# A third weight buffer for the last segment's projections, laid over the token tiles of the input norms, with a new table of shifts

## The chip, the cores and the metric

The kernel runs on one core of a Trainium2 chip. The metric is the device time of one execution in microseconds, the median of several runs. The profile is of one execution, taken by the hardware profiler; its times count from the first instruction. TensorE multiplies matrices (PE in the profile; PEld is its weight load), VectorE is DVE, ScalarE is ACT, GpSimd is POOL, and SyncE (SP) issues all transfers (DMA).

## The reference

One transformer block on 2048 tokens of width 1024: a layer norm, attention with a compressive memory, a residual, a second layer norm, a gated feed-forward of inner width 3584, a residual.

```python
h = x + A(layernorm(x))          # A: 32 heads of 32, 4 segments of 512 tokens
out = h + B(layernorm(h))

# A, for each segment s: causal attention inside the segment, and a memory of those before
p = softmax(q @ k.T * 32**-0.5 + mask); a_dot = p @ v
a_mem = (phi(q) @ M) / (phi(q) @ z + 1e-6)      # phi(t) = t + 1 if t > 0 else exp(t)
o = g * a_mem + (1 - g) * a_dot                 # g = sigmoid(beta), one for each head
M = M + phi(k).T @ v; z = z + sum(phi(k))
A = o @ wo

B = (silu(x @ w1) * (x @ w3)) @ w2
```

Inputs and weights are bfloat16.

## The kernel before, in words

**A planner writes the order.** The kernel builds a graph of operations (`Graph`), each with an engine or a choice of engines, a cost in the planner's own model, and the operations it depends on. `Graph.op` and `Graph._touch` find the dependences from the memory that operations read and write, so two tiles laid over the same place are kept apart automatically. `Graph.schedule` then plays the graph through: whenever an engine is free, it takes, among the operations that are ready, the one with the lowest pair of class (`cls`) and sequence number (`seq`). The result is a fixed order on each of the five queues (TensorE, ScalarE, VectorE, GpSimd, SyncE). `Graph.emit` writes it out with semaphore waits. On the chip nothing is reordered: a late transfer holds its queue up.

**Shifts.** Operations are counted in units: `Graph.stage` begins the next one. A table `SHIFT` gives a unit a pair (a number added to `seq`, a number added to `cls`). With it the order is moved about without touching the code that builds the graph. Classes: score bursts 0, columns and retrievals 1, projections 5, output projections 5 or 7, feed-forward up 7, feed-forward down 8; transfers have classes of their own. Units 252 to 281 are the projections of the last segment, segment 3. Unit 252 is the load of the first half of the query weights, and 253 to 256 are the four output tiles made with it; 257 with 258 to 261 are the same for keys, 262 with 263 to 266 for values; 267 to 281 repeat this for the second half.

**Stages.** `first_half` normalizes the first four token tiles and projects half of segment 0's queries, keys and values in short matmuls. `ln1(s)` loads the four token tiles of segment s into `xs0` to `xs3`, normalizes them in place (`ln`) and transposes them by DMA into `xnT[s]`. `qkv(s)` makes queries, keys and values with six weight halves of 1 MB: `weights` picks a buffer, a DMA fills it, and `project` runs four groups of eight matmuls of 512 columns. `attention` makes ten score bursts for each half of the heads (line 1101), each followed by an exponential on ScalarE (line 1115) and a causal mask on GpSimd (line 1124). `finish` makes numerators and denominators in column tiles (line 1194), the memory update (line 1029), and normalizes; for segments 2 and 3 the reciprocals go out to memory and come back spread over the partitions (`r_scr`, then `R0w` and `R`). `retrieve` reads the memory (line 1316). `wo_stage(s)` is the output projection with the second norm, whose result is transposed into `hnT[s]`. `ffn_up` and `ffn_down` are the feed-forward, in two blocks of 1024 tokens. Ordinary matmuls of all stages are recorded by one helper, `mms`, at line 747, so in the profile they are told apart by their tiles.

Projections, output projections and feed-forward matmuls are what TensorE does between the score bursts, which ScalarE's exponentials space out.

**Weight buffers.** `wp0` and `wp1` are places of their own; `wp2` lies on `oT1`, the attention output of odd segments, and so can be used by segments 0 and 1 only. `weights` counts its calls in `n_wp`, six for each segment: numbers 0 to 11 rotate over three buffers, 12 to 23 over `wp0` and `wp1`. The feed-forward's weight pairs, `w13[0]` = (`w1b0`, `w3b0`) and `w13[1]` = (`w1b1`, `w3b1`), lie at `r2` and `r2 + 8192`. At `r2` are the token tiles `xs0` to `xs3`, 2 KB each in a partition; at `r2 + 8192` is `xnT`, the normalized input of segments 0 and 3.

Of the kernel before, what the change touches and what calls it, by code (L numbers as in the profile page):

```python
# [10 lines left out]
BF16 = DT.bfloat16  # L11
# [19 lines left out]
    0: (-18, 0), 3: (-173, 0), 4: (-182, 0), 5: (1074, 0), 6: (1041, 1), 7: (-959, -1),  # L31
    8: (-283, 1), 9: (1560, 1), 10: (-14, 0), 11: (1, 0), 12: (51, -1), 13: (-257, 0),
    14: (-1703, 0), 15: (2952, 0), 16: (-2912, 0), 18: (-87, -1), 19: (3455, 1), 20: (-401, -1),
    21: (22, 0), 22: (2924, -1), 23: (-669, 0), 24: (-328, -1), 26: (-261, -1), 27: (11, -1),
    28: (-153, 0), 29: (-317, 0), 31: (1524, -1), 32: (211, 0), 33: (-1, 0), 34: (2, 0),
    35: (-15, 0), 38: (118, 1), 39: (2057, 0), 40: (223, 0), 41: (2279, -1), 42: (914, 1),
    43: (-1135, 1), 44: (2665, 1), 45: (3218, 1), 47: (1997, 1), 48: (664, -1), 49: (1928, -1),
    50: (-2800, -1), 51: (7, 0), 52: (-1130, 0), 53: (116, 0), 54: (669, 0), 55: (1018, 0),
    56: (2, 0), 57: (-289, 1), 58: (4, 0), 59: (731, 0), 60: (-304, 0), 61: (-436, 0),
    62: (64, 1), 63: (-3, 0), 64: (-63, 0), 65: (-50, 0), 66: (-174, 0), 67: (-937, 0),  # L40
    68: (808, 0), 69: (1512, -1), 70: (28, 0), 71: (-58, 1), 72: (1441, 1), 73: (-75, 1),
    74: (2141, 0), 75: (778, 1), 76: (-752, 1), 77: (90, 1), 78: (-21, 0), 79: (151, 0),
    80: (1343, 0), 81: (-1130, 0), 83: (160, 0), 84: (687, 0), 85: (-676, 0), 86: (312, 0),
    87: (-266, 0), 88: (-263, 0), 89: (-1189, -1), 90: (-164, 0), 91: (680, 1), 92: (-1801, 0),
    93: (1499, 0), 94: (3153, 0), 95: (-261, 0), 96: (0, -1), 97: (-11, 0), 98: (2, 0),
    99: (944, 0), 100: (-54, 0), 101: (1016, 0), 102: (-842, 0), 103: (147, 0), 104: (-1191, 0),
    106: (-47, 0), 107: (121, 1), 108: (-1142, 0), 109: (-1295, -1), 111: (699, 0),
    112: (-365, -1), 113: (-594, 0), 115: (28, 0), 116: (2452, -1), 117: (-8, 0), 118: (676, 0),
    119: (54, 0), 120: (-1449, -1), 121: (235, 0), 122: (-9, -1), 123: (-13, 1), 124: (45, 0),
    125: (-1279, 1), 127: (-283, -1), 129: (555, 0), 130: (1438, -1), 132: (617, 1),  # L50
    133: (81, 0), 134: (-2285, -1), 135: (-179, 0), 136: (3199, 1), 137: (389, 0),
    138: (920, 0), 139: (146, 1), 140: (687, 1), 141: (27, 0), 142: (-619, 1), 143: (1934, 1),
    144: (-922, 0), 145: (415, -1), 146: (-312, 0), 147: (-26, 0), 148: (-870, 0),
    149: (2501, 1), 150: (1682, 0), 151: (-28, 0), 152: (609, 1), 153: (611, 0), 154: (-302, 0),
    156: (0, 1), 157: (-185, 1), 158: (391, 0), 159: (-373, 0), 160: (-610, 0), 161: (-1748, 0),
    162: (-133, 0), 163: (-4056, 1), 164: (1073, 1), 166: (-202, 0), 168: (-3204, -1),
    169: (-2075, -1), 170: (2581, -1), 171: (-39, 1), 172: (-122, 1), 173: (-18, 1),
    174: (-37, 0), 175: (34, 0), 176: (1853, 1), 177: (-140, 0), 178: (-301, 0), 179: (204, 0),
    181: (165, 0), 182: (-13, 0), 183: (-7, 0), 184: (687, -1), 185: (-271, 0), 186: (-861, 1),
    187: (-616, 1), 188: (355, -1), 189: (-1449, 1), 190: (1132, 0), 191: (114, 0),  # L60
    192: (-22, 0), 193: (-464, 0), 194: (-2, 0), 195: (294, 0), 196: (18, 0), 197: (-2089, 0),
    199: (-2443, 0), 200: (248, -1), 201: (1, 0), 203: (210, 1), 204: (-1070, 0), 206: (-70, 0),
    207: (1441, 0), 208: (525, 0), 209: (839, 0), 210: (10, 0), 211: (-262, 0), 212: (894, -1),
    213: (203, 1), 214: (-359, 1), 215: (-2, 0), 216: (696, -1), 217: (-735, 0), 218: (-51, 0),
    219: (4750, 0), 220: (-465, -1), 221: (-23, 0), 222: (-196, 1), 223: (399, 0),
    224: (-1932, 1), 225: (-192, 0), 226: (-134, 0), 227: (-1542, 1), 229: (153, 1),
    230: (-676, 1), 231: (-73, 0), 232: (618, 1), 234: (-465, 0), 235: (0, -1), 237: (222, -1),
    238: (609, 0), 239: (1282, 0), 241: (-183, 1), 242: (845, 1), 243: (811, -1),
    244: (1681, -1), 246: (6, 1), 248: (-2423, -1), 249: (11, 0), 250: (21, 0), 251: (-2902, 1),
    252: (-599, 1), 253: (927, 0), 255: (308, -1), 256: (4, -1), 257: (-382, 0), 258: (30, 0),  # L70
    259: (-35, 0), 260: (-73, -1), 261: (-386, 0), 262: (-58, 1), 263: (-1713, 0),
    264: (-165, 0), 265: (-369, 1), 266: (-12, 0), 267: (808, -1), 268: (1356, 0),
    269: (-538, 0), 270: (576, -1), 272: (27, 0), 273: (609, 0), 275: (-27, 0), 277: (0, -1),
    279: (-4, 0), 280: (-3, 0), 281: (176, 0), 282: (-28, -1), 284: (-175, -1),
    285: (-1255, -1), 286: (-196, 0), 287: (308, 0), 288: (1028, 0), 289: (-18, 0),
    290: (-217, -1), 291: (628, 0), 292: (21, 0), 293: (11, 0), 294: (1042, 0), 295: (6, 0),
    296: (150, -1), 297: (222, 0), 298: (1329, 0), 299: (-799, 0), 300: (-3, 0), 301: (303, -1),
    302: (-473, -1), 303: (2419, -1), 304: (528, 0), 305: (-99, 0), 306: (2531, -1),
    307: (-28, 0), 309: (-1338, 1), 310: (-4, 1), 311: (836, 0), 312: (-154, 0), 315: (-261, 0),
    316: (443, 0), 317: (-31, -1), 318: (-1464, -1), 319: (-220, 0), 320: (340, 0),  # L80
    321: (1268, 0), 322: (-21, -1), 323: (-2755, 1), 324: (-54, 0), 325: (1643, -1),
    326: (-57, 0), 327: (1851, 0), 328: (-2912, 0), 329: (317, 1), 330: (-690, 0),
    331: (-712, -1), 332: (-940, 0), 333: (-1099, 1), 334: (-615, 1), 335: (-16, 0),
    336: (496, 0), 337: (664, 0), 338: (-166, 0), 339: (-46, 0), 340: (-700, 0), 341: (-385, 1),
    342: (-1713, 0), 344: (51, 0), 345: (-756, -1), 346: (178, -1), 348: (803, 0),
    350: (1942, -1), 351: (169, 0), 352: (-492, 1), 354: (14, 0), 355: (-39, 0), 356: (290, 0),
    357: (99, 0), 358: (-389, 0), 359: (1761, 0), 361: (1409, 0), 362: (-58, -1), 363: (550, 1),
    364: (-95, 1), 365: (-140, 1), 366: (56, 1), 367: (-11, 1), 368: (-1627, 0),
    369: (-393, -1), 370: (-2089, 0), 372: (27, 0), 373: (204, -1), 374: (-55, 0),
    375: (-622, 0), 376: (-1005, -1), 377: (-179, 0), 378: (-1188, 1), 379: (1478, -1),  # L90
    380: (-865, -1), 381: (-543, 0), 382: (-70, 0), 383: (-64, 0), 384: (-1160, 0),
    385: (-2800, 0), 386: (0, 1), 387: (-193, 1), 388: (-133, 0), 390: (2419, 0),
    391: (2201, -1), 392: (-35, -1), 394: (45, -1), 395: (-2041, 0), 396: (410, 0),
    397: (571, 1), 399: (-543, -1), 400: (-965, 0), 401: (2531, 0), 402: (-462, -1),
    403: (-129, 0), 404: (-89, 1), 405: (-60, -1), 407: (-887, 1), 408: (3072, 0),
    409: (3013, 0), 410: (1761, 1), 411: (1584, 0), 413: (281, 1), 414: (562, 0),
    415: (-1293, -1), 416: (1707, 0), 417: (-995, -1), 418: (1637, 0), 419: (-785, -1),
    420: (3, 0), 422: (-913, -1), 423: (-121, -1), 424: (-7, 0), 426: (-2, 0), 427: (-1, 0),
    430: (-1, 0), 431: (14, 0), 432: (8, 0), 433: (-33, 0), 435: (-1086, 0), 436: (72, 0),
    437: (51, -1), 438: (-293, -1), 439: (37, 1), 440: (1527, 1), 441: (-212, 0),  # L100
    442: (-3190, 1), 443: (-1357, -1), 444: (-520, 1), 445: (904, 0), 446: (-1018, -1),
    447: (697, 0), 449: (2458, 0), 450: (-40, 0), 451: (-44, 0), 452: (-8, 0), 453: (-14, 0),
    454: (658, -1), 455: (-3, 0), 456: (1, 0), 457: (-3, 0), 459: (-2315, 1), 461: (-1, 0),
    462: (539, 0), 463: (66, 0), 464: (788, 1), 465: (29, 0), 466: (24, 0), 467: (2995, 0),
    468: (-306, 1), 469: (310, 0), 470: (-30, -1), 471: (-796, 0), 472: (-70, 1),
    473: (3455, 1), 474: (62, -1), 475: (-550, 0), 476: (-2089, 0), 477: (2158, 0),
    478: (-306, 1), 479: (4, 0), 480: (1506, -1), 481: (-470, -1), 482: (3857, 0),
# [500 lines left out]
class Kernel:  # L608
# [13 lines left out]
    def plan(self):  # L622
# [37 lines left out]
        r2 = at[0]  # L660
# [264 lines left out]
    def weights(self, kind, half):  # L925

        self.g.stage()
        w = self.wp[self.n_wp % (3 if self.n_wp < 12 else 2)]
# [582 lines left out]
```

The softmax here doesn't subtract the row's maximum and nothing guards it: scores larger than these inputs give would overflow.

## Time and profile before

| | before |
|---|---|
| median of 3 runs | 888.77 us (888.38 to 888.92) |
| span of the profiled execution | 886.3 us |
| TensorE busy | 873.0 us, 5732 instructions |
| VectorE, ScalarE, GpSimd busy | 449.2, 302.5, 178.4 us |
| moved by DMA | 105.75 MB, 119 GB/s over the span |
| projection weights: loads of 1 MB | 22, of 5.6 to 7.2 us to landing (medians by matrix) |

The head lasts until the first score burst at 17.33 us; attention, with projections and then feed-forward between its bursts, until about 375 us, and the plain feed-forward until the end. The busy share of an engine is an average over these stages. What a change is worth is read from the waits of the engine that is never free, in the stage that is changed.

### The profile page before, as it was taken

The numbers are of one execution on the slowest core, as the hardware profiler recorded it, in microseconds if no ns is written. First come the engines' busy times: TensorE is split into PE (matmuls) and PEld (weight loads), VectorE is DVE, ScalarE is ACT, GpSimd is POOL, SyncE is SP. The second block draws the span as 40 slices with busy tenths as digits, with TensorE's granted clock in tenths as the row PEclk, the third lists the DMA queues.
The fourth block names the chain that finished last, engine by engine and source line by source line (L and its number), as shares of the span: only waits on it lengthen the run. The fifth ranks groups of instructions, "written<-read, shape, count | busy, mean of one in ns | idle before, by whom it ended". The sixth has DMA issues, their size and how long they took to land.

```text
span 886.3 us, 13649 instructions
## 1 busy us (share of the span) xinstructions
PE 873.0 (99%) x5732; PEld 400.5 (45%) x5821; DVE 449.2 (51%) x699; ACT 302.5 (34%) x345; POOL 178.4 (20%) x226
## 2 busy tenths in 40 slices
PE   9999999999999999999999999999999999999998
PEld 5444444444444344444444444444444444444445
DVE  6697878786665797645545301323243333341011
ACT  5878675779645555511111000101011111110000
POOL 2544443455252455303000000000000000000000
PEclk9999999999999999999999999999999999999999
DMA  7869939464862736198354410221323321301010
GB/s 238 208 185 244 227 91 267 125 156 119 217 155 74 175 83 156 53 300 258 103 156 107 120 35 30 78 65 54 83 61 88 95 72 48 90 7 41 30 54 24
DMA packets 148796, 105.75 MB, mean 119 GB/s; under 512 B 46336, under 2 KB 134400, under 8 KB 147712
## 3 DMA queue, kind: packets, MB, share of 16 engines
q1 hardware_dynamic: 148736, 104.89, 44.5%
q8 instruction: 46, 0.75, 0.4%
q14 instruction: 14, 0.11, 0.0%
HBM read 84.94 MB, written 9.44 MB: 106 GB/s over the span
## 4 chain that ended last, share of the span: by engine, by line
PE 94%; DMA 2%; DVE 2%; issue 1%; POOL 0%; ACT 0%; SPq 0%; ACTq 0%; POOLq 0%; DVEq 0%
PE ps L747 88%; PE ps L1194 3%; PE ps L1101 3%; DMA R0w<-r_scr 1%; DMA r_scr<-T 1%; DVE oT L1332 0%; SPq L1281 0%; DMA xs<-in_A_x_dram 0%; PE ps L1029 0%; DVE lnst L874 0%; ACT et L1115 0%; PE ps L1316 0%; POOL et L1124 0%; DVE hm L1397 0%; PE ps L1187 0%
## 5 line engine op out<-in xcount | busy, mean ns | idle before, releaser
L747 PE MATMUL ps<-hnT,w1b 128*128 128x512 bf16 x875 | 219.8, 379 | 2.0 <-issue 0.5
L747 PE MATMUL ps<-hnT,w3b 128*128 128x512 bf16 x879 | 217.1, 379 | 1.5 <-issue 0.5
L747 PE MATMUL ps<-w2b,hm 128*128 128x512 bf16 (+2 forms) x935 | 198.5, 366 | 0.9
L1389 ACT ACTIVATE sg<-ps 128x512 bf16<-128x512 f32 x112 | 66.8, 597 | 385.9 <-PE ps L747 385.8
L1392 DVE SCALAR_TENSOR_TENSOR t<-sg,ps 128x512 bf16<-128x512 bf16 x112 | 76.7, 685 | 183.1 <-ACT sg L1389 182.6
L1115 ACT ACTIVATE et<-ps 128x2048 bf16<-128x2048 f32 x80 | 150.0, 1874 | 45.1 <-PE ps L1101 44.7
L747 PEld LDWEIGHTS ps<-w2b,hm 128*128 128x128 bf16 x952 | 90.9, 98 | 103.0
L747 PEld LDWEIGHTS ps<-hnT,w1b 128*128 128x128 bf16 x896 | 86.2, 98 | 106.3 <-issue 6.5
L747 PEld LDWEIGHTS ps<-hnT,w3b 128*128 128x128 bf16 x896 | 86.3, 98 | 106.1 <-issue 3.6
L1124 POOL TENSOR_SCALAR_AFFINE_SELECT et<-et 128x512 bf16<-128x512 bf16 (+1 forms) x96 | 93.1, 976 | 133.0 <-ACT et L1115 132.7
L1397 DVE SCALAR_TENSOR_TENSOR hm<-t,ps 128x512 bf16<-128x512 bf16 x112 | 76.2, 685 | 40.8 <-PE ps L747 39.0
L1421 DVE TENSOR_TENSOR ob<-hr,ps 128x512 bf16<-128x512 bf16 (+2 forms) x34 | 22.2, 655 | 120.6 <-PE ps L747 120.4
L747 PE MATMUL ps<-wo,oT 128*128 128x512 bf16 x246 | 60.9, 379 | 1.1 <-issue 0.8
L747 PE MATMUL ps<-xnT,wp 128*128 128x512 bf16 (+1 forms) x345 | 59.6, 320 | 1.3 <-issue 0.8
L747 PE MATMUL ps<-hnT,wp 128*128 128x512 bf16 x249 | 59.4, 380 | 0.8 <-issue 0.6
L1138 DVE TENSOR_TENSOR sum<-sum,et 128x512 bf16<-128x512 bf16 (+1 forms) x64 | 43.6, 684 | 11.6 <-POOL et L1124 6.1
L747 PEld LDWEIGHTS ps<-xnT,wp 128*128 128x128 bf16 x352 | 28.0, 98 | 26.9 <-issue 2.8
L747 PEld LDWEIGHTS ps<-wo,oT 128*128 128x128 bf16 x256 | 23.9, 98 | 29.9 <-issue 3.3
L747 PEld LDWEIGHTS ps<-hnT,wp 128*128 128x128 bf16 x256 | 23.5, 98 | 29.7 <-issue 3.9
L1101 PE MATMUL ps<-qT,kT 32*128 32x128 bf16 (+3 forms) x512 | 31.7, 301 | 0.0
L747 PE MATMUL ps<-wp,xnT 128*128 128x512 bf16 x123 | 30.2, 379 | 0.4 <-issue 0.2
L747 PE MATMUL ps<-wp,hnT 128*128 128x512 bf16 x123 | 29.6, 380 | 0.5 <-issue 0.3
(97 smaller groups left out, 560.1 us busy)
## 6 DMA issues: line engine op xcount, KB each, us to landing
w3b<-in_B_w_dram SPq DMA_DIRECT2D x28, 512.0 KB, 4.1
w1b<-in_B_w_dram SPq DMA_DIRECT2D x28, 512.0 KB, 4.0
wp<-in_A_wv_dram SPq DMA_DIRECT2D x8, 1024.0 KB, 6.5
wp<-in_A_wq_dram SPq DMA_DIRECT2D x7, 1024.0 KB, 5.6
wp<-in_A_wk_dram SPq DMA_DIRECT2D x7, 1024.0 KB, 7.2
w2b<-in_B_w_dram SPq DMA_DIRECT2D x7, 1024.0 KB, 5.8
xs<-in_A_x_dram SPq DMA_DIRECT2D x16, 256.0 KB, 5.9
h<-in_A_x_dram SPq DMA_DIRECT2D x16, 256.0 KB, 4.0
```

The costliest lines, as they stand in the source:

```text
L747: return [e.matmul(p[0](gr), p[1], p[2], start=p[3], stop=p[4]) for p in part]
L1101: ins.append(e.matmul(self.bank(gr, j, 512 - 128 * kc, off), k[r, g0 + g, 128 * kc:128 * kc + 128], q[r, g0 + g, 128 * kc:512], start=True ...
L1115: return [e.activation(et[:, :, :], src, AF.Exp, scale=self.scale)]
L1124: self.pool_op(lambda e, v=v, pat=pat: e.affine_select(v, v, pattern=pat, compare_op=ALU.is_ge, fill=0.0, base=0, channel_multiplier=-1), ...
L1138: lambda e, gr: [e.tensor_tensor(out, x, y, op=ALU.add)], reads=[x, y],
L1194: ins.append(e.matmul(self.ps[32 * i:32 * i + 32, b * 512 + c0:b * 512 + c0 + n], lhsT(i, kc, j), rhs(i, j), start=kc == 0 and j == first, ...
L1389: self.g.op("act", act_ns(512), lambda e, gr, sg=sg: [e.activation(sg, self.bank(gr), AF.Tanh, scale=0.5)], writes=[sg], cls=0, group=gg)
L1392: e.scalar_tensor_tensor(t1, sg, 1.0, self.bank(gr), op0=ALU.add, op1=ALU.mult)], reads=[sg], writes=[t1], cls=0,
L1397: e.scalar_tensor_tensor(dst, t1, 0.5, self.bank(gr), op0=ALU.mult, op1=ALU.mult)], reads=[t1], writes=[dst], cls=0,
L1421: self.g.op("dve", dve_ns(n), lambda e, gr, hs=hs, ob=ob, n=n: [e.tensor_tensor(ob, hs, self.bank(gr, 0, n), op=ALU.add)], reads=[hs], wri ...
```

## The change

A fourth buffer object, `wp3`, is laid at `r2`, over the four token tiles, whose 8 KB in a partition it fills exactly. `weights` gives the six halves of segment 3 (numbers 18 to 23) the buffers `wp0`, `wp1`, `wp3`, `wp0`, `wp1`, `wp3`, in the order queries, keys, values of the first half and then of the second. So both value halves go to `wp3`, and a load waits until the half loaded three before it is used up, where it was two before it. The token tiles are done with when segment 3's input has been transposed. `w13[0]`, which lies there as well, can be loaded only when the last value projection has read `wp3`.

The table of shifts is new throughout, 517 entries in place of 535; only entries that the text speaks of are shown.

```diff
 SHIFT = {
...
-    252: (-599, 1), 253: (927, 0), 255: (308, -1), 256: (4, -1), 257: (-382, 0), 258: (30, 0),
-    259: (-35, 0), 260: (-73, -1), 261: (-386, 0), 262: (-58, 1), 263: (-1713, 0),
...
-    279: (-4, 0), 280: (-3, 0), 281: (176, 0), 282: (-28, -1), 284: (-175, -1),
...
+    251: (-179, 1), 252: (2460, 0), 253: (-124, 0), 254: (6, 0), 255: (-23, 0), 256: (106, 1),
+    258: (21, 1), 259: (2, 1), 260: (52, 0), 261: (116, 0), 262: (3, -1), 266: (186, -1),
...
+    273: (0, 1), 274: (27, 0), 275: (868, 0), 276: (2554, 0), 277: (-895, 0), 279: (661, 0),
+    280: (605, 1), 281: (415, 0), 284: (1451, 1), 285: (168, -1), 286: (-20, 0), 287: (431, 0),
...
         self.wp.append(buf("wp2", [128, 8, 512], BF16, self.g.base[self.oT[1].name][1]))
+        self.wp.append(buf("wp3", [128, 8, 512], BF16, r2))
...
     def weights(self, kind, half):
 
         self.g.stage()
-        w = self.wp[self.n_wp % (3 if self.n_wp < 12 else 2)]
+        w = self.wp[(0, 1, 3)[self.n_wp % 3] if self.n_wp > 17 else self.n_wp % (3 if self.n_wp < 12 else 2)]
         self.n_wp += 1
```

## The prediction

> **What bounds the kernel now.** I read the page's busy line first, then the chain that ended last, then the waits of TensorE after the start-up, then TensorE's order of time around the longest of them, and last the weight loads.
>
> ```profile
> PE 873.0 (99%) x5732; PEld 400.5 (45%) x5821; DVE 449.2 (51%) x699; ACT 302.5 (34%) x345; POOL 178.4 (20%) x226
> PEclk9999999999999999999999999999999999999999
> PE 94%; DMA 2%; DVE 2%; issue 1%; POOL 0%; ACT 0%; SPq 0%; ACTq 0%; POOLq 0%; DVEq 0%
> ```
>
> TensorE is busy for 873.0 of 886.3 us at full clock, and 94% of the chain is its own work. Busy time alone would not prove saturation, so here are its waits from 17 us to the end (us in total, times, longest):
>
> ```profile
> PE ps L747 <- issue: 3.7, 23, 0.2
> PE ps L1316 <- DMA R<-r_scr: 0.8, 1, 0.8
> PE ps L747 <- DVE hm L1397: 0.4, 1, 0.4
> PE ps L747 <- ACT sg L1389: 0.3, 1, 0.3
> PE ps L1194 <- POOL et L1124: 0.3, 1, 0.3
> ```
>
> and pieces of its order of time (start, length, then the instruction):
>
> ```profile
> 73.22 0.39 PE L1101 MATMUL ps<-qT,kT 32*128 32x512 bf16 x4
> 73.78 0.81 PE L747 MATMUL ps<-hnT,wp 128*128 128x512 bf16 x3 [0.16 <-issue]
> 74.42 1.03 PE L747 MATMUL ps<-wp,xnT 128*128 128x512 bf16 x4
> ...
> 297.18 1.03 PE L747 MATMUL ps<-hnT,w3b 128*128 128x512 bf16 x4
> 299.05 0.44 PE L1316 MATMUL ps<-pq,Mbf 32*32 32x512 bf16 x16 [0.85 <-DMA R<-r_scr]
> ```
>
> The 3.7 us of "issue" are not real. Projections come in fours, and each such row has x3 (or 7, or 11): a record is missing, and the hole is one matmul long. What is left are four waits, 0.8 + 0.4 + 0.3 + 0.3 = 1.8 us. Taken from start to start instead of from modelled ends, they and three smaller ones (at 257.7, 457.5 and 727.0 us) come to 0.91 + 0.54 + 0.36 + 0.31 + 0.13 + 0.37 + 0.06 = 2.7 us.
>
> The rest closes by counting. From the first score burst at 17.33 us to the last matmul's end at 883.98 us are 866.65 us. In these run 3680 full matmuls (the code's 1792 + 896 of the feed-forward, 256 of the output projection, 768 of the projections, less 32 in the head; narrower pieces counted by columns). In the plain feed-forward stretch the chain's steps begin at 374.61 and 385.40 us, 50 matmuls apart: 215.8 ns each, so 794 us. 80 score bursts at 0.43 us (58.00 to 58.43: 0.10 to go over to row tiles, 0.21 of work, 0.12 to come back) are 34 us, 8 column blocks at 3.6 to 4.2 us about 32, and 6 retrievals at 0.42 about 2.5. The sum is 863; with 2.7 of waits it is 866. **All that a new order can remove behind the head is 2.7 us, and some tenths where a burst comes to lie beside a column block and saves one change of tiling.** In the head, TensorE's real work (32 transposes and 128 short matmuls, about 9.1 us) begins at 6.63 and ends at 17.33: 1.6 us of idle, tied to the arrival of the four token tiles and their norms.
>
> Now the resource that the change adds to, weight buffers. First the waits on the tile wp with the time from issue to landing, and the page's row of the feed-forward's loads (KB each, us to landing):
>
> ```profile
> DMA wp<-in_A_wq_dram: 1.0, 3
> DMA to landing us min/median/max: 5.1/6.6/9.3
> ...
> w3b<-in_B_w_dram SPq DMA_DIRECT2D x28, 512.0 KB, 4.1
> w1b<-in_B_w_dram SPq DMA_DIRECT2D x28, 512.0 KB, 4.0
> ```
>
> Then single loads in the issuing queue's order of time:
>
> ```profile
> 146.87 0.56 SPq L322 DMA_DIRECT2D w3b<-in_B_w_dram  x1
> 147.53 1.14 SPq L322 DMA_DIRECT2D w1b<-in_B_w_dram  x1
> ...
> 223.81 0.38 SPq L322 DMA_DIRECT2D wp<-in_A_wv_dram  x1
> 224.23 0.58 SPq L322 DMA_DIRECT2D wp<-in_A_wk_dram  x1
> ```
>
> And TensorE where the projections end and the feed-forward begins:
>
> ```profile
> 247.92 1.03 PE L747 MATMUL ps<-xnT,wp 128*128 128x512 bf16 x4
> 248.78 1.03 PE L747 MATMUL ps<-hnT,w1b 128*128 128x512 bf16 x4
> ```
>
> The only waits on a projection weight are 1.0 us in the first microseconds. Segment 3, with two buffers, never holds TensorE up.
>
> **What the Trainium skill says.** "TensorE: Matmul & The Clock Gate", section "Wait — 56ns, not 53.3ns?", gives about 215.7 ns from start to start for a warm matmul of 512 columns; the trace's 215.8 ns agrees, so these matmuls have no slack inside. "Perfetto Trace Analysis", section "Identifying the Most-Contended Engine", warns that matmul busy share is a poor measure; hence the count above. Its section "Optimization Strategy" says that consistent bubbles on the saturated engine can mean too few buffers. The trace of before shows no such bubble in segment 3.
>
> **The change, part by part.**
>
> The third buffer. Segment 3's six loads go to buffers 0, 1, 3, 0, 1, 3 in place of 0, 1, 0, 1, 0, 1. Bytes and matmuls stay. The value half-matrices get wp3, so they need not wait for a query or key buffer. Removed from TensorE: 0 us, as it waits for none of these loads now. Its own load waits for the token tiles' last transpose, issued by 141 us in the trace of before, well ahead of segment 3's value load at 205.85: 0 us.
>
> The place of wp3. It lies on the token tiles, where w1b0 and w3b0 of the feed-forward lie too. Those two are fetched at 147 us now, 101 us ahead of use. After the change they wait for the last value projection of segment 3, and the other pair (on the segment's normalized input) waits, as now, for the last projection of any kind. On the queue of the issuing engine, whatever is issued behind that waiting load waits too: norm outputs, h tiles and row copies. Cost if exposed: one 512 KB landing, 4.0 us, plus 0.6 us to issue the second. It is hidden if other projections follow the values. The new entries speak for that: query tile 256 and key tiles 258 and 259 of the first half are moved one class back, so buffers 0 and 1 come free late, and the second half's query and key loads (landing 5.6 and 7.2 us by the median) follow. The values need neither buffer. Eight groups of eight matmuls (8 x 1.73 = 13.8 us) then stand behind them and hide 4.6 us. Against it: value tile 280 is moved one class back as well, and could be the last. I take 0 us, with 4.6 as the other end.
>
> The new shifts. They alter nearly every priority, hence the order on all five queues. Work and tile sizes remain, so TensorE's sum remains, apart from waits and changes of tiling. I count none of the old seven waits as kept; the new order will have its own, where a real transfer or evacuation comes later than the planner thought. In the old order 350 us of dense interleaving left 2.3 us of them (the rest lie in the feed-forward). With no reason in the trace for the new one to be better or worse fitted, I take about 2.3 again, with 0.5 and 5 as ends; a small credit of 0.3 us for the freer weight loads, since the largest wait is on a row copy that shares the queue with them. The head's chain (tiles, norms, transposes) is the same work with the same arrivals: 0, from -1 to +0.5. The tail stays: the last token tile is still last, with its 256 and 128 column pieces.
>
> Sum: 888.8 + 0 + 0 - 0.3 = **888.4 us**.
>
> **The rivals.**
>
> *The waits are cleared.* Nearly all of the 2.7 us goes, or half of them and a microsecond of the head. For it: the longest wait is a single one of 0.9 us, and freer buffers make orders possible that were not. Against it: the weights cause none of the waits, and the order has to fit better everywhere at once. 888.8 - 2.5 = 886.3 us.
>
> *New late arrivals.* The fresh order puts several needs closer to real landings than the planner thinks: landings of projection weights range from 5.1 to 9.3 us, and a key transpose takes 5.3 by its median. Three more waits like the 0.9 us one, none of which other work fills since TensorE's order is fixed: 888.8 + 2.7 = 891.5 us. For it: nothing in the code measures the chip. Against: the old order, made in the same manner, has only one wait over 0.6 us.
>
> *The lost prefetch shows.* A value projection is the last of segment 3, and the feed-forward has no weights: 888.8 + 4.6 = 893.4 us. Against it: the order of the shifts above, and the output projection of segment 1 (64 matmuls, 13.8 us), which can fill as well.
>
> **How the numbers follow.** Forecast 0.49, cleared waits 0.25, late arrivals 0.19, lost prefetch 0.07. The bound of 0.2% is 1.8 us. Faster by more needs two thirds of all that can be removed: 0.25. Slower: 0.26. Between: 0.49. For the range, I reach down to 886.2, just past the cleared-wait case, and up to 891.6, just past the late arrivals; outside lie the lost prefetch and the tails of the others, about 0.2.
>
> **What would show it.** Right: TensorE's busy time within 2 us of 873.0; no wait of a projection on wp after the head; w1b0 and w3b0 issued after the last value projection and landed before the first feed-forward matmul; feed-forward steps still 215.8 ns apart; waits from start to start between 1 and 4 us. Wrong: an idle stretch of some microseconds between the last projection and the first w1b matmul (lost prefetch); several waits of about a microsecond on row copies, transposes or evacuations (late arrivals); or a body with almost no wait and a first score burst before 16.5 us (cleared).

## The result, and the profile after

The changed kernel takes **892.17 us** (median of 4 runs, 891.70 to 893.03), the kernel before 888.58 us beside it: the ratio is 1.0043, with an interval of 1.0025 to 1.006. It is slower by 3.6 us. The profiled executions differ by 4.6 us (spans of 890.9 and 886.3 us). The changed code starts its lines four earlier, so `mms` is line 743 here, the row copies are line 1277, the memory update is line 1025.

The page of the changed kernel: the busy line, and by engine the chain that ended last.

```profile
PE 881.8 (99%) x5821; PEld 399.7 (45%) x5821; DVE 444.4 (50%) x701; ACT 300.6 (34%) x340; POOL 181.9 (20%) x229
...
PE 91%; DMA 6%; DVE 1%; ACT 1%; SPq 0%; issue 0%; POOL 0%; DVEq 0%
```

TensorE has all of its 5821 matmul records here, 89 more than the page of before, and that is most of why its busy time is longer; it does the same matmuls. What has changed is the chain: 6% of it now lie in transfers, where it was 2%. That share isn't lost time: where a wait of half a microsecond ends with a landing, the chain takes in the whole transfer (behind the wait of 0.39 us at 91 us lie 13.71 us of it). The loss is read from the waits. The waits of TensorE from 17 us to the end do (us in total, times, longest):

```profile
PE ps L743 <- DMA w3b<-in_B_w_dram: 1.2, 2, 0.8
PE ps L743 <- ACT lnst L718: 0.8, 1, 0.8
PE ps L743 <- DMA wp<-in_A_wk_dram: 0.5, 1, 0.5
PE ps L743 <- ACT v L766: 0.5, 1, 0.5
PE ps L743 <- DMA wp<-in_A_wv_dram: 0.4, 1, 0.4
PE ps L1312 <- DMA R<-r_scr: 0.4, 1, 0.4
PE ps L1190 <- POOL et L1120: 0.2, 1, 0.2
```

The old waits for hm and sg are gone, those for R and for the mask (et) are shorter, and six new ones have come. They are waits for quite different things: projection weights, an evacuation (v) and a step of the norm (lnst) on ScalarE, feed-forward weights. Two pieces of TensorE's order of time, and the load behind the second:

```profile
237.97 1.89 PE L743 MATMUL ps<-xnT,wp 128*128 128x512 bf16 x8
240.64 1.02 PE L743 MATMUL ps<-wo,oT 128*128 128x512 bf16 x4 [0.78 <-ACT lnst L718]
...
750.30 1.03 PE L743 MATMUL ps<-hnT,w3b 128*128 128x512 bf16 x4
752.09 2.12 PE L743 MATMUL ps<-hnT,w3b 128*128 128x512 bf16 x9 [0.76 <-DMA w3b<-in_B_w_dram]
```

```profile
745.31 0.37 SPq L317 DMA_DIRECT2D w3b<-in_B_w_dram  x1
```

The w3b load is issued at 745.31 us; the order wants it some 6 us later, at 751.3, and it is there at 752.1. From issue to landing these loads take 4.7 us by the median, so the order looked safe; this one took longer.

A wait is now taken from the start of one matmul to the start of the next, less what that step takes elsewhere. Added up in this way, the span comes out for every profile whose granted clock stayed at 1.00; five are shown. "First scores" is the start of the first score burst; the last column, "rest", is the span less the first two and less 0.6 us for the changed order's six extra changes of tiling (194 against 188, at 0.10 us; three blocks of column matmuls are now split):

| profile | span | first scores | waits after 17 us | rest |
|---|---|---|---|---|
| before | 886.3 | 17.3 | 2.7 | 866.3 |
| changed | 890.9 | 18.4 | 5.7 | 866.2 |
| changed, run again (e7) | 893.2 | 18.0 | 8.3 | 866.3 |
| changed, eleven moves (e5) | 888.1 | 18.6 | 2.9 | 866.0 |
| before, six moves (e12) | 885.1 | 17.2 | 1.4 | 866.5 |

The rest is the same to half a microsecond. So the 4.6 us are 3.0 of waits, 1.0 of a later start of attention and 0.6 of changes of tiling.

### The profile page after: what moved, and what is told of

The parts are those of the page before. It is cut to its first block, busy times and chain, and to the rows that moved or that the text cites. A ratio compares the mean times of both kernels' runs of the same rounds, so it can differ in the third digit from the quotient of the medians.

```text
span 890.9 us, 13717 instructions
## 1 busy us (share of the span) xinstructions
PE 881.8 (99%) x5821; PEld 399.7 (45%) x5821; DVE 444.4 (50%) x701; ACT 300.6 (34%) x340; POOL 181.9 (20%) x229
## 4 chain that ended last, share of the span: by engine, by line
PE 91%; DMA 6%; DVE 1%; ACT 1%; SPq 0%; issue 0%; POOL 0%; DVEq 0%
PE ps L743 85%; PE ps L1190 3%; PE ps L1097 2%; DMA wp<-in_A_wv_dram 2%; DMA w3b<-in_B_w_dram 1%; DMA R<-r_scr 1%; DMA xs<-in_A_x_dram 1%; DMA wp<-in_A_wq_dram 1%; DMA wp<-in_A_wk_dram 1%; ACT et L1111 0%; SPq L1277 0%; PE ps L1025 0%; PE ps L1312 0%; DMA r_scr<-T 0%; DVE lnst L870 0%
## 5 line engine op out<-in xcount | busy, mean ns | idle before, releaser
L1120 POOL TENSOR_SCALAR_AFFINE_SELECT et<-et 128x512 bf16<-128x512 bf16 x96 | 91.8, 963 | 126.7 <-ACT et L1111 126.7
L743 PE MATMUL ps<-wo,oT 128*128 128x512 bf16 x256 | 62.9, 379 | 0.8 <-ACT lnst L718 0.8
L743 PE MATMUL ps<-xnT,wp 128*128 128x512 bf16 (+1 forms) x352 | 61.7, 321 | 1.7 <-DMA wp<-in_A_wq_dram 0.9
L1134 DVE TENSOR_TENSOR sum<-sum,et 128x512 bf16<-128x512 bf16 (+1 forms) x64 | 40.9, 638 | 14.0 <-POOL et L1120 10.2
L1328 POOL TENSOR_TENSOR oT<-Nsb,R 128x512 bf16<-128x512 f32 x23 | 31.3, 1387 | 12.2 <-DVE R L1325 12.2
L1134 DVE TENSOR_TENSOR sum<-et,et 128x1024 bf16<-128x1024 bf16 x32 | 28.0, 876 | 9.6 <-ACT et L1111 8.7
L1357 DVE TENSOR_TENSOR h<-h,ps 128x512 bf16<-128x512 bf16 x32 | 21.9, 684 | 21.5 <-PE ps L743 21.1
```

The lines of the kernel that those rows point to most:

```text
L743: return [e.matmul(p[0](gr), p[1], p[2], start=p[3], stop=p[4]) for p in part]
L1120: self.pool_op(lambda e, v=v, pat=pat: e.affine_select(v, v, pattern=pat, compare_op=ALU.is_ge, fill=0.0, base=0, channel_multiplier=-1), ...
L1134: lambda e, gr: [e.tensor_tensor(out, x, y, op=ALU.add)], reads=[x, y],
L1328: self.either(lambda e, out=out, Ns=Ns, R1=R1: e.tensor_tensor(out, Ns, R1, op=ALU.add), 512, 2, [Ns, R1], [out], 2)
L1357: self.g.op("dve", dve_ns(512), lambda e, gr, hs=hs: [e.tensor_tensor(hs, hs, self.bank(gr), op=ALU.add)], reads=[hs], writes=[hs], cls=1, ...
```

## The experiments

Two ways to alter the order were used. A kernel with *moves* takes the order that the planner has found and puts single operations a few places earlier (negative) or later on their queue; everything else stays in its place. An entry of `MOVES` gives the queue, the first operation, how many are moved, and by how many places. A *replay* gives the planner another kernel's order as priorities, and its choice of engines, in place of the table of shifts.

### e1 and e2: take the waits away by moves

```diff
+MOVES = [
+    ('sp', 1049, 1, 7),
...
+    ('sp', 1154, 3, -5),
+    ('pe', 2358, 1, -12),
...
+    ('pe', 1345, 1, 4),
...
+]
```

> The new kernel, same buffers and shifts; after planning, 14 moves of a few places each inside single queues (TensorE groups behind a transfer or evacuation that comes late are exchanged with neighbours, row copies go earlier). No work is added or left out. Theory A (the loss is made of waits of TensorE on late needs): the waits at 90.7, 129.8, 232 to 240, 306.8, 751 and 774 us of the new kernel's trace, together about 3.7 us from start to start, shrink to about 0.8, and the time goes from 892.2 to about 888.9, no slower than the kernel before by more than 0.7. Rival B (the overlay of wp3 costs the time, by transfers held back): the time stays within 0.7 us of 892.2.

> The kernel before, with 10 such moves at its own waits (264 to 308 us and 728 us). Theory A: its waits of 0.91 us on a row copy, 0.36 on an evacuation and 0.54 on the feed-forward's evacuation go, the time falls from 888.6 to about 887.0. If the waits are not what costs the time, it stays at 888.6.

Neither got faster. e1: 893.71 us, ratio to before 1.006 (1.0047 to 1.0072), which isn't told from the changed kernel's 1.0025 to 1.006. e2: 890.81 us, ratio 1.0017 (1.001 to 1.0023), slower than before. Neither theory had this. In e1 nearly all of the planned waits did go, but one R0w copy that had been put seven places later was issued at 248.01 us in place of 246.4. The product that needs it, in the changed kernel and in e1:

```profile
252.82 1.75 DVE L1292 TENSOR_TENSOR Nsb<-Nsb,R0w 128x512 f32<-128x512 f32 x1
```

```profile
256.99 2.37 DVE L1335 TENSOR_TENSOR Nsb<-Nsb,R0w 128x512 f32<-128x512 f32 x2 [6.17 <-DMA R0w<-r_scr]
```

With it VectorE's next products came late: a new wait of TensorE of 2.34 us at 259.6. In e2 the fourth R copy went out 0.85 us later, and the wait for it grew from 0.91 to 2.28 us. Both copies looked idle because no engine was seen waiting for them; they had no slack all the same. (The wait in e2 isn't the same in every execution: nine of its 21 runs took 889.0 to 890.0 us, twelve 890.8 to 892.2. The profile, 891.0, is one of the twelve.)

There is a second cost. The stretch around e2's wait (from and to in us, its length, busy time and count of PE, PEld, DVE, ACT and POOL, then PEclk, DMA share, GB/s):

```profile
...
300.00:301.00 1.00, 0.00 (x0) 0.00 (x0) 0.00 (x0) 0.00 (x0) 0.00 (x0) 1.00 1.04 238
301.00:302.00 1.00, 0.98 (x17) 0.27 (x18) 0.16 (x1) 0.00 (x0) 0.23 (x1) 0.56 0.78 180
302.00:304.00 2.00, 2.00 (x6) 0.75 (x5) 1.34 (x2) 0.47 (x1) 0.59 (x2) 0.50 0.04 8
304.00:306.00 2.00, 2.00 (x9) 0.84 (x8) 1.81 (x3) 0.30 (x2) 2.00 (x3) 0.87 0.57 161
```

After the wait the clock that TensorE is granted is one half for 3.4 us: 0.44 + 2 x 0.50 + 2 x 0.13 = 1.7 us more are lost behind a wait of 2.3.

### e3: without the new shifts of the tail

```diff
 SHIFT = {
...
-    572: (339, 0), 573: (-414, 0), 574: (3, 0), 575: (-2315, -1), 576: (1158, 0),
...
-    589: (-1091, 0), 591: (4206, 0), 592: (2477, 1), 593: (1282, 0), 594: (1426, 0),
...
+    571: (833, -1), 572: (339, 0), 593: (1282, 0), 594: (1426, 0), 595: (-905, 1), 596: (2868, 0),
...
```

> The new kernel without the shifts of units 573 to 592, the last chunks of the second block's feed-forward up; the order is the new kernel's up to 726 us. Theory A: both waits on w3b (0.93 and 0.55 us) go, and nothing else changes: 892.2 - 1.5 = 890.7 us. Rival B: 892.2, as the third buffer is long free by then.

891.93 us, ratio 1.0035 (1.0022 to 1.0047). In the profile both waits for w3b are gone and nothing has come in their place, as theory A has it; but the time, 2.8 us over the 889.17 of before beside it, is not clearly shorter than the changed kernel's. By time alone this run decides nothing.

### e4 and e10: the buffer without the shifts, the order without the buffer

```diff
-        for o in ops:
-            late, cls = SHIFT.get(o.unit, (0, 0))
-            o.seq += late + 1e-6 * o.seq
-            o.cls += cls
+        for i, o in enumerate(ops):
+            o.cls, o.seq, o.engs = 0, RANK[i] + 1e-6 * i, (ENGINES[ENG[i]],)
...
```

`RANK` is the other kernel's order and `ENG` its engines: in e4 the order of before in the changed code (the up product of the first two feed-forward chunks is held behind the gate product), in e10 the changed order in the code of before, with the changed kernel's places in PSUM as well.

> The third buffer alone: the new kernel's buffers, and the kernel before's order as priorities in place of the shifts (in the first two chunks, the w3 group may not take a bank before its w1 group). Theory A: in the old order the value projections are among the last of segment 3, so w1b0 and w3b0, fetched at 147 us before, can be fetched only at 248 us; TensorE runs out of work for at least 4.6 us, and the time is 893 to 903 us. If the overlay is harmless by itself in any order: 888.6 us, within 1.

> The kernel before, with its two weight buffers and its token tiles for the input norms, and the new kernel's order as priorities: the order without the buffer. Where the plan needs the third buffer it goes its own way. Theory A (the third buffer by itself wins no time; the order holds the loss): 891 to 894 us, like the changed kernel. Rival B (the order lives on the third buffer: with two, the weights of the last segment come late): a wait of 2 us or more for a wp load after 165 us, and 895 us or more. Rival C (the loss is the buffer's): under 890.

e4: 903.79 us, ratio 1.017 (1.0151 to 1.0188). TensorE in e4, in order of time:

```profile
253.98 1.03 PE L898 MATMUL ps<-xnT,wp 128*128 128x512 bf16 x4
259.98 0.66 PE L1467 MATMUL ps<-pq,Mbf 32*32 32x512 bf16 x16 [4.98 <-DMA R<-r_scr]
262.29 3.34 PE L898 MATMUL ps<-hnT,w1b 128*128 128x512 bf16 x8 [1.65 <-DMA w1b<-in_B_w_dram]
```

With wp3 on their place, w1b0 and w3b0 are loaded at 251.8 us and not at 147. In the order of before, feed-forward matmuls fill the time until the row copies are there; here there are none to fill it, so the retrieval waits 5.0 us and the first feed-forward matmul another 1.65. The prefetch that the buffer costs is worth much in that order. Not all of e4's 14.6 us are the lost prefetch: it also has waits for exponentials of 1.0 and 2.3 us at 204 and 207 us, and the granted clock is one half for 3.4 us behind these and for 6.8 us in the stretch shown.

e10: 910.49 us, ratio 1.024 (1.0206 to 1.0274). The time is rival B's. Its mechanism is seen in part only: three projections wait for their weights after 165 us, but by 0.9, 0.3 and 0.9 us, none by 2. More is lost where the plan has nothing to put between score bursts:

```profile
200.59 0.40 PE L1305 MATMUL ps<-qT,kT 32*128 32x128 bf16 x8
202.97 0.40 PE L1305 MATMUL ps<-qT,kT 32*128 32x512 bf16 x4 [1.99 <-ACT et L1319]
205.35 0.40 PE L1305 MATMUL ps<-qT,kT 32*128 32x128 bf16 x8 [1.98 <-ACT et L1319]
```

Four bursts stand one behind the other from 200.6 us on, and each after the first waits for the exponential of one before it. Just ahead of them, at 198.75 us, a projection waits for its weights, so the plan may have had no projection ready because two buffers were full; the trace doesn't show that. Replayed alone, the buffer costs 14.6 us and the order 21.8; together they cost 3.6. So the new order makes good most of what the buffer's place costs in the old one. (A replay isn't a new table: shifts found for the code of e4 or of e10 could do better. That wasn't tried.)

### e5 and e7: moves on the compute engines alone, and the changed kernel again

```diff
+MOVES = [
+    ('pe', 1349, 1, 1),
+    ('pe', 2461, 1, -1),
+    ('pe', 2358, 1, -12),
+    ('pe', 1802, 1, 5),
+    ('pe', 344, 1, 1),
+    ('pe', 329, 1, -2),
+    ('pe', 574, 1, -2),
+    ('pe', 1345, 1, 4),
+    ('pe', 1344, 1, 3),
+    ('pe', 2365, 1, 2),
+    ('act', 534, 1, 5),
+]
```

> The changed kernel with eleven small moves in TensorE's and ScalarE's order and none in the queue of loads, so that no load or row copy is issued in another place. They put ready work ahead of the first matmul that waits at 90.7, 129.8, 239.5, 259.9, 467.6, 751 and 774 us. Theory A (what the new kernel lost is the waits that its order leaves, and the first moved kernel failed only because one R0w row copy, moved back four places, brought a 2.3 us wait of its own and a slower TensorE clock behind it): these waits fall from 3.9 us to about 1.0, no wait above 1.5 us appears, the granted clock stays 1.000, and the time is 892.2 - 2.9 = 889.3 us (888.7 to 890.3). Rival B (the loss is not in these waits; they move elsewhere as soon as one is filled): the time stays at 892.2 +- 0.7 and new waits of the same sum are seen.

> The changed kernel once more, with nothing altered, for the spread of its waits from one execution to the next and for its time beside the others of this call. If the later start of attention (18.37 us in the profile against 17.33) is the order's, the first scores are again at 17.8 us or later; if it was the landing of the loads in that one execution, they can fall at 17.3. The waits for w3b near 751 and 774 us, for the ScalarE evacuation at 239.5 and for wk at 129.8 should be there again, with a sum of 3.0 +- 0.5. The stall inside the memory update at 181 us, where nothing waited for is recorded, was 0.28 us, and 1.04 and 1.44 in two edited kernels: anything from 0 to 1.5. Time 892.2 (891.5 to 893).

e7: 893.62 us, ratio 1.0052 (1.0039 to 1.0064), 0.6 us above the interval that was expected. e5: **890.71 us**, ratio 1.0019 (1.0013 to 1.0026). The moves win 2.9 us over the changed kernel measured beside it, which is what theory A had; the time itself is 0.4 us above its interval, since the changed kernel was slower here too. Waits in e7:

```profile
...
PE ps L1312 <- DMA R<-r_scr: 1.9, 2, 1.3
PE ps L743 <- DMA w3b<-in_B_w_dram: 1.4, 3, 0.7
PE ps L1025 <- issue: 0.9, 1, 0.9
PE ps L743 <- ACT lnst L718: 0.8, 1, 0.8
...
```

and in e5:

```profile
...
PE ps L1065 <- issue: 1.2, 1, 1.2
PE ps L783 <- ACT v L806: 0.3, 1, 0.3
PE ps L1230 <- POOL et L1160: 0.2, 1, 0.2
PE ps L783 <- DVE t L1428: 0.2, 1, 0.2
PE ps L1137 <- ACT et L1151: 0.2, 1, 0.2
```

The waits for w3b, wp, R and the norm on ScalarE are gone. What is left is the stall called "issue" and four small ones. Nothing but the places of eleven operations differs, so the waits of the order are most of the loss: 2.9 us of the 4.5 by which the changed kernel is slower here. What e5 keeps is the later first scores and the six changes of tiling. e7 shows besides that a wait in the changed kernel is not a fixed number: the R copy at 257 us cost nothing in the first profile and 1.4 us in this one.

### e8: the stall that nothing explains

One wait is called "issue": TensorE waited for nothing that the trace names. In e7 it lies inside the memory update, behind a burst of short column matmuls:

```profile
179.31 0.72 PE L1190 MATMUL ps<-et,v 128*32 128x512 bf16 x16
179.85 0.65 PE L1025 MATMUL ps<-v,pkn 128*32 128x33 bf16 x59
181.40 0.22 PE L1025 MATMUL ps<-v,pkn 128*32 128x33 bf16 x5 [0.90 <-issue]
```

```diff
+MOVES = [
+    ('pe', 802, 1, 2),
+]
```

> The changed kernel with one move: the memory update at 181 us, 64 matmuls of 8 ns, comes after the two projection groups that followed it, so that 1.7 us of long matmuls stand between it and the burst of short column matmuls ahead of it. Theory A (the stall inside it is TensorE's instructions coming in too slowly, in a burst of some 175 matmuls in 4 us beside loads at 160 to 320 GB/s): no stall of over 0.1 us among the memory matmuls. Rival B (it is a wait of the memory update for something that the trace does not name): the stall goes with the update to its new place. The time changes by -0.3 to +0.2 us, less than can be told.

The same place in e8:

```profile
180.00 1.67 PE L773 MATMUL ps<-wp,hnT 128*128 128x512 bf16 x7 [0.16 <-issue]
181.61 0.56 PE L1055 MATMUL ps<-v,pkn 128*32 128x33 bf16 x51
182.46 0.27 PE L1055 MATMUL ps<-v,pkn 128*32 128x33 bf16 x13 [0.30 <-issue]
```

The time, 893.84 us, is the changed kernel's. Neither theory had it quite. The stall is shorter (0.47 us from start to start against 1.07), but it is there; and it comes after 51 matmuls of the update, not after 59. Two groups of four matmuls were put ahead of it, so it is at the same *instruction*. In all six profiles of the changed kernel and of its edits by moves and by e3, TensorE has begun 1741 weight loads when it goes on. A wait for data would have moved with the update. A fixed count of instructions fits the edge of a block of instructions that has to be fetched. The Trainium skill, "Runtime: NRT & Kernel Launch", section "Instruction fetch mechanics", says that instructions come in blocks of 16 KiB by a queue of their own, while the engine runs, and that crossing a block's edge is mostly hidden. The queue is in the trace. From 176 to 182 us, in the kernel before and in e7 (packets, MB, share of 16 engines over the 6 us):

```profile
q8 instruction: 2, 0.03, 2.2%
```

```profile
q8 instruction: 1, 0.02, 2.0%
```

One packet of 16 KB takes 1.1 us before (2.2% of 96 us, for two), 1.0 us in the changed kernel's first profile, where the stall was 0.28 us, and 1.9 us in e7, where it was 1.07. In the same way it is 1.7 us in e3 (stall 1.04) and 2.2 us in e5 (1.38). And TensorE goes on 1.2 to 1.5 us after this packet has ended, in all six profiles, late or early as it is (179.95 and 181.27 us in the changed kernel, 180.12 and 181.40 in e7, 181.08 and 182.46 in e8). That ties the stall to the packet. There are 46 such packets in a trace, and a wait of over half a microsecond without a named cause is seen behind this one alone; elsewhere the traces agree that the edges are mostly hidden. In the kernel before, no transfer ran while its packet came (176.5 to 177.5 us); in the new order two 1 MB weight loads start at the burst (177.79 and 178.21 us) and move 303 GB/s from 179 to 181 us. That the loads slow the packet is a reading from these profiles, and not the whole of it: the packet took 1.0 us in the changed kernel's first profile, with 238 GB/s moving beside it, and 1.7 us in e3, with 203. A kernel with the loads elsewhere wasn't tried, since the first of them is wanted 6.5 us after its issue and takes 6.0 us to land.

### e9: the head

```diff
...
-            o.cls += cls
+        for i, o in enumerate(ops):
+            o.cls, o.seq, o.engs = 0, RANK[i] + 1e-6 * i, (ENGINES[ENG[i]],)
...
```

Here `RANK` is the changed order, with the operations of the first 17.3 us in the order of before; places in PSUM are given as in e10.

> The changed kernel with the order of the kernel before in the first 17.3 us alone (transposes and 128-column products of the first segment, on TensorE, VectorE and ScalarE, and their PSUM banks); the rest is planned after it with the new kernel's order as priorities, and stands in another order in places up to 280 us. Theory A (the new order asks for the key weights too early: in six profiles of it the first scores came 7.5 us after wk had landed, at 10.3 to 11.1 us, while in four profiles with the old head they came at 17.2 to 17.4 whatever the landing, 10.46 to 10.62): first scores at 17.2 to 17.5 us, and no wait for wk near 10.4. Rival B (landing differs from execution to execution and the order is innocent): first scores at 17.8 or later. The time gets 0.6 shorter by A, 892.5, give or take 1 us for the waits that the other order up to 280 us has instead.

The new order asks for the key weights early. In the changed kernel:

```profile
10.00 0.62 PE L743 MATMUL ps<-xnT,wp 128*128 128x128 bf16 x8
10.92 0.62 PE L743 MATMUL ps<-xnT,wp 128*128 128x128 bf16 x8 [0.30 <-DMA wp<-in_A_wk_dram]
```

and in e9, at the same point of the head:

```profile
10.16 1.07 PE L952 MATMUL ps<-xnT,wp 128*128 128x128 bf16 x16
11.06 0.61 PE L964 MATMUL ps<-ident,xs 128*128 128x128 bf16 x8
```

There the wait for wk is gone. The first scores came at 18.05 us, which by the number is rival B's; but all head loads landed late in this execution (wq at 8.53, wk at 11.00 us). So they are set against the landings. With the new head the first scores come 7.5 us after wk's landing in all six profiles (10.30 to 11.10, and 17.80 to 18.59). With the old head in e2, e4 and e6 they come 9.3 us after wq's, at 17.24 to 17.41, with wk at 10.48 to 10.62; e9 is at 7.05 after wk and 9.5 after wq. (In the kernel before and in e11, where wq landed sooner, at 7.32 and 7.45, they came at 17.33 and 17.26 all the same, so the old head hangs on more than wq.) Compare e4 and e7, with all but equal landings (wk at 10.59 and 10.51): 17.39 and 18.00. So 0.6 us of the head is the order's by this pair, and the rest of the first profile's 1.0 is the landing.

As a kernel e9 is far off: 917.21 us, ratio 1.0318 (1.0289 to 1.0347). Only the head was to change, but what comes first decides what is ready next, and up to 280 us the planner went another way, with 8.6 us of waits for exponentials alone. This order could not be joined from halves.

### e6, e11 and e12: is there a kernel that beats both?

Moves in the kernel before, none on the queue of loads. e6 has eight, two of them on VectorE; e11 has three of these, e12 six, and no VectorE move. The six of e12:

```diff
+MOVES = [
+    ('pe', 1432, 1, -3),
+    ('pe', 1366, 1, 2),
+    ('act', 1185, 1, 4),
+    ('pe', 2343, 1, 1),
+    ('pe', 1435, 1, -2),
+    ('pe', 1191, 1, -1),
+]
```

> The kernel before with eight small moves on TensorE, VectorE and ScalarE, and none of the two moves of R row copies that the earlier moved kernel had. Theory A (waits are the loss, and the earlier one got slower because its fourth R copy was issued 0.75 us later and a 2.3 us wait slowed the clock): the waits at 266 us (0.36) and 308.7 us (0.54) go, the wait for the R copy stays between 0.3 and 0.9, and the time is 1.2 us under the kernel before, 888.0 (887.4 to 888.8). Rival B: the same as before or slower, with the wait for R at 2 us or more again.

> The kernel before with three moves only: two on TensorE and one on ScalarE, none on VectorE. Theory A (in the earlier set of eight moves it was the VectorE moves that put a 1.48 us pq scaling between two oT products and so made hm 2.4 us late; TensorE's own moves do what they should): the wait at 266 us (0.36) goes and the wait for the R copy at 298 us falls from 0.91 to 0.7 or less, hm stays at 0.5 to 0.8; the time is 0.2 to 0.8 us under the kernel before of the same call. Rival B (any move in this stretch gives back what it wins): the same as before within 0.3 us, or slower, with a wait for hm of 1.5 us or more.

> The kernel before with the same three moves and three more on TensorE (the feed-forward products behind hm at 306 to 309 us come in another order), again none on VectorE. Theory A: the waits at 266, 298 and 308.7 us, 1.8 us together before, come to 0.8 or less, and the time is 1.0 us under the kernel before (0.4 to 1.4). Rival B: a wait for hm of 1.5 us or more, and the same time or slower.

e6: 891.89 us, ratio 1.0024 (1.0012 to 1.0037): the time is rival B's, but not by its wait for R, which had gone. VectorE in the kernel before (two of its lines), and in e6:

```profile
300.38 0.42 DVE L1003 TENSOR_SCALAR pq<-qT 128x1024 bf16<-128x1024 bf16 x1
...
308.74 0.67 DVE L1397 SCALAR_TENSOR_TENSOR hm<-t,ps 128x512 bf16<-128x512 bf16 x1
```


```profile
306.87 1.74 DVE L1369 TENSOR_TENSOR oT<-Nsb,R 128x512 bf16<-128x512 f32 x1 [0.66 <-POOL Nsb L1333]
308.53 1.48 DVE L1040 TENSOR_SCALAR pq<-qT 128x1024 bf16<-128x1024 bf16 x1
309.94 1.75 DVE L1369 TENSOR_TENSOR oT<-Nsb,R 128x512 bf16<-128x512 f32 x1
311.61 0.67 DVE L1434 SCALAR_TENSOR_TENSOR hm<-t,ps 128x512 bf16<-128x512 bf16 x1
```

The moved pq scaling took 1.48 us here, 0.42 in its old place at 300.38, and it stands ahead of hm now. hm starts 2.9 us later than before (311.61 against 308.74), half of it by the scaling and half because the oT products begin 1.5 us later. TensorE, without the wait for R, asks for it only 0.9 us later: its wait grows from 0.54 to 2.53 us, with the slower clock behind. Without the VectorE moves: e11 888.41 us, ratio 0.9992 (0.9984 to 1.0), e12 **887.72 us**, ratio 0.9984 (0.9975 to 0.9994), with 889.46 for the kernel before beside both. The interval of e11 reaches 1, so it isn't told from the kernel before; e12 is faster, by 0.5 to 2.2 us. The waits left in e12:

```profile
PE ps L782 <- issue: 3.5, 22, 0.2
PE ps L782 <- DMA wp<-in_A_wq_dram: 0.6, 1, 0.6
PE ps L1229 <- POOL et L1159: 0.3, 1, 0.3
PE ps L782 <- DVE Macc L1080: 0.2, 1, 0.2
```

The waits for R, sg and hm are gone, as theory A had it (as in the prediction, the 3.5 us of "issue" are missing records). e12 beats both kernels, with two buffers and six moves of one to four places; it is the best of four sets of moves, and its gain is small.

## Why the prediction was wrong, point by point

**Right.** TensorE is the bound, and behind the head only waits and changes of tiling can be won or lost: the last column of the table is the same for both kernels. (Two small readings were off and change nothing: the last matmul ends at 883.88 us, not 883.98, and a fifth wait of 0.2 us, for Macc, was left out of the list.) The place of wp3: w1b0 and w3b0 were issued at 201.10 and 201.97 us, their first matmul ran at 232.8, projections filled until 256.8. The values came first, as read from the shifts, and the lost prefetch cost 0. The third buffer won 0: no projection of segment 3 waits on wp3, and none did before. (e4 shows how near the other end was: in the order of before TensorE waits 5.0 and 1.65 us where the prefetch is missing.)

**Wrong: "I take about 2.3 again"**, the step on the new shifts, for the waits of the interleaved part, with 0.4 us in the feed-forward. They measured 4.0 and 1.7 us. This is the term of the sum that was mis-sized, by 3.0 us with both parts, and e5 shows it: eleven moves of the order bring back 2.9 us. The ends were 0.5 and 5, so the interleaved part lay within; the feed-forward's waits had no range of their own, and the prediction has no reason why the plain stretch should keep its 0.4. Two of its own signs failed with it: projections waited for weights after the head (0.55 us at 91 and 0.65 at 130 us), and the waits came to more than 4 us. The causes are the ones of the rival "new late arrivals" (an evacuation, weights that land late, a row copy), whose sum of three waits of 0.9 us was about right. It got 0.19, for the reason that the old order has only one wait over 0.6 us. That was a sample of one order and one execution; in e7 the changed kernel itself had 8.3 us of waits in place of 5.7.

**Wrong: the head, "0, from -1 to +0.5".** It measured +1.0 in the first profile and +0.7 in the second; 0.6 of it is the order's (e4 against e7, e9). The work is the same, as said, but not the load that it hangs on: wk in place of wq.

**Not counted.** Six more changes of tiling, 0.6 us: the text allowed for saving one, not for splitting column blocks. And the credit of 0.3 us for freer loads isn't to be seen: the waits for R copies are 0.45 us in the first profile, but 2.1 in e7, against 0.91 before.

Together the waits (1.7 + 1.3), the head (1.0), the tiling (0.6) and the credit (0.3) are 4.9 us, the distance from the forecast (0.3 us under before) to the profile (4.6 us over). The range ended at 891.6, at the rival's own 891.5, and was 0.6 us short; with the head's own bad end of 0.5 added it would still have missed, by 0.1.

## What to carry to other kernels

Where an order is written ahead and an engine is full, a new order's cost is its waits, and how many it has can't be read from the old order's waits: give it a wide and one-sided range, since there is much more to lose than to win. A buffer that no engine waits for wins nothing by itself, and if it takes the place of a prefetch, the order must be made anew for it. To win the last tenths, move a few operations of the full engine past a wait seen in the trace, and read the new trace. The sets that held (e5, e11, e12) moved TensorE and one ScalarE operation; those that moved a transfer or VectorE as well (e1, e2, e6) lost what they had won, because an operation that nobody is seen waiting for may still have no slack.

## What the runs showed of the hardware

**A wait of over 2 us can cost 1.7 us more, and whether it does depends on where it falls.** In e1, e2 and e6 (waits of 2.34, 2.28 and 2.53 us) the granted clock then stood at 0.50 for 3.41 us. After waits of 1.4 us (e5, e7) it stayed at 1.00, but so it did in e9 after a wait of 2.75 us:

```profile
PE ps L952 <- DMA wp<-in_A_wq_dram: 2.8, 1, 2.8
```

The clock records of the traces show why. Within an execution the clock changes only at whole steps of 3.41 us from one change to the next: in e10 at 168.61, 172.03, 206.16 and 212.99 us, which is 1, 10 and 2 steps apart. In six profiles (e1, e2, e4, e6, e9, e10) it fell to one half nine times, each time behind a step in which TensorE was busy for 0.0 to 1.42 us. Behind every step with 1.65 us or more a full clock stayed full. The wait in e9, from 116.50 to 119.25 us, was cut by a step's edge at 118.16 us into 1.66 and 1.09 us. The Trainium skill, "TensorE: Matmul & The Clock Gate", section "Part 1: The HAM clock gate", puts the half clock after at least one idle window of about 3.4 us; here less was enough.

**Instruction fetch can stall TensorE.** So the profiles read, though no run moved the fetch itself. At a fixed instruction, in a burst of some 175 short matmuls in 4 us beside loads at 300 GB/s, it cost 0.28 to 1.44 us in six profiles; the kernel before has the same burst with no loads beside it, and no stall.

**The same VectorE instruction took 0.42 us in one place and 1.48 us in another** (the pq scaling at line 1003 of before, line 1040 of e6). The traces say more: it runs 168 times in the fourteen profiles. All 66 that took longer than 0.5 us (0.72 to 1.49) began while a GpSimd instruction was running; of the other 102 (0.41 to 0.46 us), 91 began with GpSimd idle. That is a coincidence in time over many cases, and no run took the GpSimd work away.
